# A fused attention and two-MLP kernel: the load of the third weight slice issued behind the first pair of heads' transposes

## Chip, cores and metric

One core of one Trainium2 chip runs the whole program as one launch. The metric is the device time of that launch in microseconds (us). Three runs of the kernel before gave 974.56, 975.61 and 974.90 us; the median is 974.9 us.

## What is computed

A causal attention with a learned decay (4 batches, 8 heads, 576 positions, head size 64) feeds an MLP with a squared relu (512 to 2048 and back), and that feeds a gated MLP (512 to 1536 and back), all in float32, with 2304 tokens:

```python
scores = scale * (q @ k.T)                       # per batch and head
cum    = cumsum(maximum(s, 0))
scores = where(causal, -1e9, scores + minimum(-(cum[:, None] - cum[None, :]), 0))
attn   = exp(scores - max(scores)); attn /= sum(attn) + 1e-9
x      = merge_heads(attn @ v)                   # 2304 x 512

h = maximum(x @ w_in, 0)
x = (s * h * h + b) @ w_out

out = ((x @ w_a) * (x @ w_b)) @ w2_out
```

The products keep float32 accuracy by splitting operands into a high and a low part and adding three products (high with high, high with low, low with high). Such splits are the bulk of the work of ScalarE (ACT) and VectorE (DVE).

## The kernel before

The program is written as a list of operations with an engine, a cost and a priority each (`Plan.op`, L79). `Plan.order` (L125) plays this list through with its own costs and writes out one fixed order, in which every engine then runs its instructions one behind the other. An operation can name others that it must be issued behind (`behind`, kept in the field `then`); it also becomes eligible only when its buffers have room. The buffers of one tag (`Tag`, L34) are handed out in the order in which they were declared, unless the tag says otherwise. A change to one operation can therefore move many others.

The first stretch, some 150 us, does two things at once.

**Attention, first halves.** Eight groups of four heads; group i is loaded by `light_load(i)` (L388): the keys and queries of the group (`kq`, two transfers of 64 x 1024, L411), its values (`rv`, L412) and two rows of running sums (L416). `first_half(i)` (L615) treats the group as two pairs of heads. For each pair, in two tiles of query rows (ti = 1 and 0): TensorE (PE) makes the scores `s` (L645), DVE their maximum `nm` (L650), ACT the exponentials `p` (L661), ACT and DVE the high and low part `hl` of the scaled probabilities (L555, L557), and a DMA transposes `hl` into `tr` (L671). One more PE operation, `av` (L595), multiplies `tr` with the values. ACT (L606) and DVE (L608) split its result into `x_all`. Names carry batch, pair and tile: `s0031` is the scores of batch 0, pair 3, tile 1, and `av003` and `tr003` belong to batch 0, pair 3. Groups 0 and 1 (`kq0`, `kq1`) are batch 0, groups 2 and 3 are batch 1.

**First MLP.** The weights come in 16 slices of 1 MB (`raw0` to `raw15`), loaded by `split_w` and `decode` (L479, L447, the load on L459). The inputs are 64-bit words; ACT and DVE put them together (L463, L468 or L472, L474), ACT or GpSimd (POOL) rounds to the high part (L483) and DVE makes the low part (L484). Only then can PE use a slice, in `h` (L934, which needs all four pairs of a batch) and `y` (L954).

Even slices and the early `kq` tiles share one tag, with 16 slots, in the order of declaration: `raw0`, then `raw2`, then `kq2`, `kq3`, then the first finished slice. Odd slices use a single buffer of their own, so slice f + 2 is loaded only when slice f is finished (odd f).

All transfers named here are issued by SyncE (SP), one behind the other, on one queue. Eight semaphores are used in turn: a transfer is issued only when the one issued eight places earlier has landed. The order on SP around the change is `raw0`, `raw1`, `raw2`, the loads of group 2, one load of group 3, and then the four transposes of the first two pairs.

Of the kernel before, what the change touches and what calls it, by code (L numbers as in the profile page):

```python
# [30 lines left out]
PE, DVE, ACT, POOL, SP = "PE", "DVE", "ACT", "POOL", "SP"  # L31
# [207 lines left out]
def fused_kernel(  # L239
# [15 lines left out]
    nc = tc.nc  # L255
# [12 lines left out]
    plan = Plan()  # L268
    op = plan.op
# [97 lines left out]
    def split_v(v3, rv, eng, cost, sub, pr):  # L367
# [11 lines left out]
           r=[rvb, (buf, 1)], w=[(buf, 2)])  # L379
        return ops  # L380

    light = {}
    casts = []
    last_rows = []
# [3 lines left out]
    def light_load(i, in_w):  # L388

        b, g = divmod(i, 2)  # L390
        kq = Buf(t_w if in_w else t_kq0, f"kq{i}")
        rv = Buf(t_rv0, f"rv0{i}")
        pr = 2.0 * i if i < 2 else light_pos(i) - 8.0
        vt = Buf(t_vt0, f"vt0{i}")
        light[i] = kq, rv, vt

        def view():
            a = kq.t.bitcast(F32).rearrange("p a b n -> p a (b n)") if in_w else kq.t.rearrange("p a x h n -> p a (x h n)")
            return a

        kq.view = view
        hs = slice(b * H + 4 * g, b * H + 4 * g + 4)

        def ones():
            nc.gpsimd.memset(view()[64:66, 1], 1.0 / SCALE)
            nc.gpsimd.memset(view()[64:66, 0], -1.0 / SCALE)

        op(POOL, 1.9, pr, ones, w=[(kq, "o0"), (kq, "o1")], behind=casts[2 * i - 3 : 2 * i - 2])
        for j, src in enumerate((kl, ql)):
            op(SP, 0.5, pr + 0.1 * j,  # L410
               lambda j=j, src=src: nc.sync.dma_start(view()[0:64, j], src[b, :, g]), w=[(kq, j)], dma=360000, behind=last_rows[-1:], slack=i > 1)  # L411
        op(SP, 0.45, pr + 0.3, lambda: nc.sync.dma_start(  # L412
            rv.t.rearrange("p x c h d -> p x (c h d)"), v[b, 2 * g : 2 * g + 2, :, :2].rearrange("x p c h d -> p x (c h d)")
        ), w=[rv], dma=262144, behind=last_rows[-1:] if i else (), slack=i > 1)
        for j, row in ((0, 64), (1, 65)):
            last_rows.append(op(SP, 0.6, pr + 0.4 + 0.1 * j, lambda j=j, row=row: nc.sync.dma_start(  # L416
                view()[row : row + 1, j].rearrange("p (h n) -> p h n", h=4), sums_ap()[hs, S : S + N]
            ), r=[(sums, "cum")], w=[(kq, f"o{j}")], dma=4096, behind=last_rows[-1:]))
        casts.extend(split_v((vt, lambda a: vt.t[..., a, :]), (rv, lambda: rv.t), POOL, 0.63, 0.7, light_pos(i) + (0.5 if i else 2.6)))

    def light_pos(i):
# [25 lines left out]
    def decode(raw, src, shift_on_act, pr, load_pr, later=()):  # L447
# [11 lines left out]
            nc.sync.dma_start(a, src.bitcast(U32))  # L459

        lo, hi, hi32 = (lambda: words(0)), (lambda: words(1)), (lambda: words(1).bitcast(F32))
        op(SP, 0.42, load_pr, load, w=[raw], dma=1 << 20, behind=later, slack=True)
        op(ACT, 1.07, pr, lambda: nc.scalar.activation(  # L463
            hi32(), hi32(), AF.Prelu, scale=2.0**-112, alpha=-(2.0**32)
        ), w=[(raw, "hi")])
# [149 lines left out]
    def first_half(i):  # L615
# [8 lines left out]
        for x in range(2):  # L624
# [41 lines left out]
            for ti in (1, 0):  # L666
                w, bank, at, view, hl = tiles[ti]
                for h in range(2):
                    split_p(hl, lambda hl=hl, h=h: hl.t.rearrange("p (k a h) n -> p k a h n", a=2, h=2)[:, :, :, h],
                            pts[ti, h], (rc, at + h), w, pr)  # L670
                op(SP, 1.25, pr, lambda ti=ti, tr=tr, hl=hl: nc.sync.dma_start_transpose(  # L671
                    out=tr.t.rearrange("p (k q) -> p k q", q=N)[:, : 4 * (ti + 1), (1 - ti) * P : (2 - ti) * P],
                    in_=hl.t.rearrange("p k n -> p (k n)"),
                ), r=[hl], w=[(tr, ti)], dma=49152 * 4 * (ti + 1), late=-0.9)
            value_product(b, 0, p, vt, lambda j, h, vi, x=x: vt.t[:, x, j, h, vi, :], tr, pr + 1.0)

    for i in range(2 * B):
        first_half(i)

    save_rows()  # L680

# [1020 lines left out]
```

## Time and profile before

| what | value |
|---|---|
| median of three runs | 974.9 us |
| the profiled execution, its own time | 973.57 us |
| its span (first to last instruction) | 971.7 us |
| PE busy | 940.7 us (97%) |
| DVE busy | 732.0 us (75%) |
| ACT busy | 560.8 us (58%) |
| POOL busy | 176.4 us (18%) |
| chain that ended last, by engine | PE 86%, DVE 6%, DMA 3%, ACT 2%, issue 2%, POOL 1% |
| PE busy in the first 48 us | 29.5 us |

How to read it: the span is 1.87 us shorter than the execution's own time, and that execution was 1.33 us faster than the median. PE is nearly always busy, so the end moves only if PE waits less, or runs the same work in less time. In the page's 40 slices PE shows 5 and 7 tenths in the first two and 9 tenths in nearly all others.

### The profile page before, as it was taken

To read this page: it belongs to the slowest core of one execution; us is meant where nothing else is said; L and a number is where in the kernel's file an instruction comes from. 1 tells how busy PE (TensorE), PEld (TensorE's weight loads), DVE (VectorE), ACT (ScalarE), POOL (GpSimd) and SP (SyncE) were. 2 spreads that over 40 slices of the span, in tenths; PEclk is the share of its full clock that TensorE was granted. 3 is DMA by queue.
4 is the path that set the end of the run, shared out by engine and by line. 5 is a ranking of instruction groups with operands and counts; after the bars stand their busy time and mean duration, and the time that the engine had idled before them with its cause. 6 is when DMAs were issued, how large, how long until landed. Compare 5 with 4: busy or idle time off the path is not lost.

```text
span 971.7 us, 16847 instructions
## 1 busy us (share of the span) xinstructions
PE 940.7 (97%) x6360; PEld 762.8 (78%) x6360; DVE 732.0 (75%) x1228; ACT 560.8 (58%) x1038; POOL 176.4 (18%) x234
## 2 busy tenths in 40 slices
PE   5799999999999999999999998999999999999998
PEld 4598999999999999999988884455554544788888
DVE  6889875767988988888559628868788786978852
ACT  4777864567878787887466425364455542334431
POOL 4124123210201102003032003141243410000000
PEclk9999999999999999999999999999999999999999
DMA  9969656347778887877352300445475668986022
GB/s 246 233 161 232 208 191 139 85 135 144 170 166 169 163 162 172 155 149 165 70 195 87 109 1 1 150 165 200 168 284 206 215 240 285 349 338 225 13 71 103
DMA packets 159857, 163.25 MB, mean 168 GB/s; under 512 B 115104, under 2 KB 125088, under 8 KB 153888
## 3 DMA queue, kind: packets, MB, share of 16 engines
q1 hardware_dynamic: 159776, 162.18, 58.9%
q8 instruction: 50, 0.82, 0.3%
q14 instruction: 31, 0.25, 0.1%
HBM read 99.39 MB, written 36.47 MB: 140 GB/s over the span
## 4 chain that ended last, share of the span: by engine, by line
PE 86%; DVE 6%; DMA 3%; ACT 2%; issue 2%; POOL 1%; SPq 0%; DVEq 0%; POOLq 0%; ACTq 0%
PE b L1245 21%; PE y L954 14%; PE h L934 14%; PE pb L1492 11%; PE yy L1002 5%; PE hh L990 4%; PE av L595 4%; PE s L645 3%; PE s L831 3%; PE bc L1245 3%; PE pbc L1552 2%; DMA tr<-hl 2%; DVE hl L557 1%; DMA raw<-in_w_dram 1%; DVE x L1176 0%
## 5 line engine op out<-in xcount | busy, mean ns | idle before, releaser
L954 PE MATMUL y<-g,w 128*128 128x256 f32 x1344 | 180.3, 286 | 0.2 <-ACT p L661 0.2
L934 PE MATMUL h<-x_all,w 128*128 128x256 f32 x1344 | 178.4, 286 | 1.9 <-DVE w L484 1.5
L934 PEld LDWEIGHTS h<-x_all,w 128*128 128x128 f32 x1344 | 168.0, 193 | 3.7 <-DVE w L484 2.6
L954 PEld LDWEIGHTS y<-g,w 128*128 128x128 f32 x1344 | 167.0, 191 | 2.8 <-ACT p L661 0.4
L1245 PEld LDWEIGHTS <-wa 128*128 128x128 f16 x720 | 70.0, 98 | 57.4 <-issue 3.2
L1245 PEld LDWEIGHTS <-ws 128*128 128x128 f16 x576 | 55.9, 98 | 66.9
L555 ACT ACTIVATE hl<-p,rc 128x256 f16<-128x256 f32 (+3 forms) x128 | 65.3, 557 | 25.9 <-DVE rc L572 9.9
L557 DVE SCALAR_TENSOR_TENSOR hl<-p,rc,hl 128x256 f16<-128x256 f32 (+3 forms) x128 | 73.6, 618 | 3.6 <-ACT hl L555 3.5
L1245 PE MATMUL b<-x,wa 128*128 128x512 f16 x288 | 68.7, 379 | 0.0
L884 ACT ACTIVATE r<-h 128x512 f32<-128x512 f32 x56 | 33.1, 591 | 51.3 <-PE h L934 50.4
L595 PE MATMUL av<-tr,vt 128*64 128x320 f16 (+4 forms) x800 | 48.1, 275 | 10.3 <-DMA tr<-hl 9.4
L595 PEld LDWEIGHTS <-vt 128*64 128x64 f16 (+1 forms) x800 | 40.5, 117 | 18.6 <-issue 7.5
L1492 PE MATMUL pb<-g,wo 128*128 128x512 f32 x216 | 50.9, 390 | 1.3 <-DVE g L1440 1.3
L645 PE MATMUL s<-kq 66*128 66x256 f32 (+1 forms) x128 | 42.4, 458 | 10.0 <-DMA kq<-sums 7.5
L1245 PE MATMUL b<-x0d,ws 128*128 128x512 f16 x216 | 50.9, 379 | 0.0
L1245 PE MATMUL b<-x1d,ws 128*128 128x512 f16 x216 | 50.9, 379 | 0.0
L895 DVE SCALAR_TENSOR_TENSOR r<-r,sb_s 128x512 f32<-128x512 f32 x40 | 30.3, 757 | 25.3 <-ACT r L884 24.8
L1492 PEld LDWEIGHTS pb<-g,wo 128*128 128x128 f32 x216 | 40.4, 188 | 10.1 <-DVE g L1440 1.7
L1286 DVE TENSOR_TENSOR su<-b,su 128x512 f32<-128x512 f32 x48 | 33.0, 687 | 18.4 <-PE b L1245 15.2
L1002 PE MATMUL yy<-gg,w 128*128 128x512 f32 x192 | 46.0, 390 | 0.0
L990 PE MATMUL hh<-x_all,w 128*128 128x512 f32 x192 | 46.0, 389 | 0.0
L1300 ACT COPY su<-b 128x512 f32<-128x512 f32 x24 | 14.0, 585 | 53.4 <-PE b L1245 50.2
(416 smaller groups left out, 1864.4 us busy)
## 6 DMA issues: line engine op xcount, KB each, us to landing
raw<-in_w_dram SPq DMA_DIRECT2D x16, 1024.0 KB
raw<-in_w2ab_dram SPq DMA_DIRECT2D x12, 1024.0 KB
ab_dr<-at_all SPq DMA_DIRECT2D x24, 512.0 KB
R<-ab_dr SPq DMA_DIRECT2D x24, 512.0 KB
wo<-wo_dr SPq DMA_DIRECT2D x12, 1024.0 KB
rk<-in_k_dram SPq DMA_DIRECT2D x16, 576.0 KB
raw_o<-in_w2o_dram SPq DMA_DIRECT2D x6, 1024.0 KB
wo_dr<-wao SPq DMA_DIRECT2D x24, 256.0 KB
```

The source lines that it names most:

```text
L555: nc.scalar.activation(o, i_, AF.Copy, scale=r_)
L557: nc.vector.scalar_tensor_tensor(out=o, in0=i_, scalar=r_, in1=place()[:, k0:k1, 0, :cols], op0=ALU.mult, op1=ALU.subtract)
L595: nc.tensor.matmul(ap.t[64 * h : 64 * h + 64, :w], vap(j, h, vi), t[:, j, a, h, :w], start=j == 0 and m == 0, stop=j == nkt - 1 and m == l ...
L645: nc.tensor.matmul(o, qt[:66, x, h, ti * P : (ti + 1) * P], kt[:66, x, h, :w], start=True, stop=False)
L884: op(ACT, 0.49, e, lambda: nc.scalar.activation(r.t.rearrange("p a n -> p (a n)"), hp.t, AF.Relu), r=[hp], w=[r], late=0.1)
L934: nc.tensor.matmul(o, w[:, wi, c, :], x_t[ck, c].t[:, xi], start=m == 0, stop=m == 3 * KC - 1)
L954: nc.tensor.matmul(o, w1_t[2 * fp + j].t[:, 1, wi, e * P : (e + 1) * P], g.t[:, gi, j], start=fp == 0 and e % 2 == 0 and j == wi == gi == ...
L990: nc.tensor.matmul(hp.t, w[:, wi, c, :], x_all[:, :, c, xi, :], start=m == 0, stop=m == 3 * KC - 1)
L1002: nc.tensor.matmul(y_ps[e].t, w1_t[f].t[:, 1, wi, e * P : (e + 1) * P], g.t[:, gi].rearrange("p a n -> p (a n)"), start=f == m == 0, stop= ...
L1245: nc.tensor.matmul(o, wt.t[:, q, wi, kt * P : (kt + 1) * P], hl_of(kt, xi), start=first and n == 0, stop=last and n == 5, skip_group_check ...
L1286: op(DVE, 0.64, e, lambda: nc.vector.tensor_tensor(out=dst(), in0=bank.t, in1=a(), op=ALU.add), r=[bank, *reads], w=[key], late=0.08)
L1492: nc.tensor.matmul(banks[bi][dp].t, wv(i2, wi, dp), hl.t[:, i2, xi, :], start=n_ in fresh and ip == i2 == m == 0, stop=ip == NIP - 1 and i ...
```

## The change

The issue of the load of `raw2` waits until the transpose of tile 0 of batch 0, pair 0 has been issued. The two dictionaries only keep hold of the operations; the loads of `kq` are recorded too, and nothing is done with them.

```diff
@@
+    loads, turns = {}, {}
@@ light_load
+        n0 = len(plan.ops)
         for j, src in enumerate((kl, ql)):
...
+        loads[f"kq{i}"] = plan.ops[n0:]
@@ decode
-        op(SP, 0.42, load_pr, load, w=[raw], dma=1 << 20, behind=later, slack=True)
+        loads[raw.name] = [op(SP, 0.42, load_pr, load, w=[raw], dma=1 << 20, behind=later, slack=True)]
@@ first_half
-                op(SP, 1.25, pr, lambda ti=ti, tr=tr, hl=hl: nc.sync.dma_start_transpose(
+                turns[b, p, ti] = op(SP, 1.25, pr, lambda ti=ti, tr=tr, hl=hl: nc.sync.dma_start_transpose(
@@
     for i in range(2 * B):
         first_half(i)
+
+    for name, p in (("raw2", 0), ):
+        for o in loads[name]:
+            turns[0, p, 0].then.append(o)
+            o.wait += 1
```

The order that the planner writes differs from there on, on every engine; on PE the two orders run alike again from about the thousandth row. Three places of it follow, before and after.

SP, from the first weight slice to the transposes of the second pair. Before:

```order
L459 DMA raw0_149<-in_w1_dram 128x2048
L459 DMA raw1_152<-in_w1_dram 128x2048
L459 DMA raw2_160<-in_w1_dram 128x2048
L411 DMA kq2_162<-in_kl_dram 64x1024
L411 DMA kq2_162<-in_ql_dram 64x1024
L412 DMA rv02_177<-in_v_dram 128x2x256
L416 DMA kq2_162<-sums_111 1x4x256 x2
L411 DMA kq3_224<-in_kl_dram 64x1024
L671 DMA_TRANSPOSE tr000_245<-hl0001_144 128x8x128
L671 DMA_TRANSPOSE tr000_245<-hl0000_155 128x4x128
L671 DMA_TRANSPOSE tr001_267<-hl0011_169 128x8x128
L671 DMA_TRANSPOSE tr001_267<-hl0010_180 128x4x128
```

With the change:

```order
L462 DMA raw0_149<-in_w1_dram 128x2048
L462 DMA raw1_152<-in_w1_dram 128x2048
L414 DMA rv02_160<-in_v_dram 128x2x256
L674 DMA_TRANSPOSE tr000_227<-hl0001_144 128x8x128
L674 DMA_TRANSPOSE tr000_227<-hl0000_155 128x4x128
L462 DMA raw2_245<-in_w1_dram 128x2048
L413 DMA kq2_247<-in_kl_dram 64x1024
L413 DMA kq2_247<-in_ql_dram 64x1024
L674 DMA_TRANSPOSE tr001_274<-hl0011_165 128x8x128
L674 DMA_TRANSPOSE tr001_274<-hl0010_173 128x4x128
L418 DMA kq2_247<-sums_111 1x4x256 x2
L413 DMA kq3_271<-in_kl_dram 64x1024
```

The third slice takes the keys and queries of group 2 with it, since their buffers stand behind its buffer in the shared tag; they now lie between the transposes of pair 0 and those of pair 1.

DVE, behind the low parts of pair 1. Before:

```order
L472 TENSOR_SCALAR raw2_160<-raw2_160 128x1024
L484 TENSOR_TENSOR w1_0_262<-raw0_149,w1_0_262 128x2x512
L571 TENSOR_SCALAR rc002_279<-sm002_253 128x4
L572 RECIPROCAL rc002_279<-rc002_279 128x4
L525 CAST sums_hl_282<-sums_111 32x576
L527 TENSOR_TENSOR sums_hl_282<-sums_111,sums_hl_282 32x576
L474 SCALAR_TENSOR_TENSOR raw1_152<-raw1_152 128x1024
L557 SCALAR_TENSOR_TENSOR hl0021_200<-p00210_252,rc002_279,hl0021_200 128x2x128
```

With the change:

```order
L653 TENSOR_REDUCE nm003_277<-s0031_253 128x2
L653 TENSOR_REDUCE nm003_277<-s0030_265 128x2
L657 TENSOR_SCALAR nm003_277<-nm003_277 128x4
L574 TENSOR_SCALAR rc002_311<-sm002_241 128x4
L575 RECIPROCAL rc002_311<-rc002_311 128x4
L487 TENSOR_TENSOR w1_0_309<-raw0_149,w1_0_309 128x2x512
L611 SCALAR_TENSOR_TENSOR x_all_82<-av000_283,x_all_82 128x256
L560 SCALAR_TENSOR_TENSOR hl0021_191<-p00210_240,rc002_311,hl0021_191 128x2x128
```

The maxima of pair 3 come ahead of the weight work; before they stood behind the low parts of pair 2, because PE made `s0030` only after `av000`. The steps on `raw1` and `raw2` go back.

PE, around the first `h`. Before:

```order
L595 MATMUL av100_574<-tr010_500,vt02_361 64x128
L934 MATMUL h0_0_597<-x_all_82,w1_0_262 128x256 x12
L934 MATMUL h0_0_597<-x_all_82,w1_1_363 128x256 x12
L645 MATMUL s0130_646<-kq3_224 128x128
L646 MATMUL s0130_646<-mask1_84,ident_83 128x128
```

With the change:

```order
L649 MATMUL s0120_524<-mask1_84,ident_83 128x128
L942 MATMUL h0_0_535<-x_all_82,w1_0_309 128x256 x12
L942 MATMUL h0_0_535<-x_all_82,w1_1_469 128x256 x12
L648 MATMUL s0131_611<-kq3_271 128x256
L649 MATMUL s0131_611<-mask1_84,ident_83 128x128
```

The first `h` stood behind all of `s0131` and `av100` before; now it stands behind `s0120`, ahead of both. In the whole order ahead of it, one score tile of 256 columns and one `av` are missing.

## Rows read from the trace of the kernel before

**Rows 1.** The page: busy time of each engine; granted clock in 40 slices.

```profile
PE 940.7 (97%) x6360; PEld 762.8 (78%) x6360; DVE 732.0 (75%) x1228; ACT 560.8 (58%) x1038; POOL 176.4 (18%) x234
...
PEclk9999999999999999999999999999999999999999
```

**Rows 2.** Windows: stretch, length, busy PE, PEld, DVE, ACT, POOL, clock, DMA share, GB/s.

```profile
14.00:16.00 2.00, 2.00 (x7) 1.73 (x7) 1.34 (x6) 0.56 (x2) 0.06 (x1) 1.00 1.00 422
...
24.00:36.00 12.00, 9.12 (x61) 8.05 (x61) 9.80 (x19) 8.88 (x25) 3.06 (x4) 1.00 0.80 162
36.00:48.00 12.00, 7.51 (x44) 5.94 (x44) 9.79 (x24) 9.48 (x29) 0.00 (x0) 1.00 1.03 299
48.00:60.00 12.00, 12.00 (x81) 10.87 (x78) 8.79 (x19) 6.38 (x18) 4.98 (x5) 1.00 0.83 209
60.00:72.00 12.00, 12.00 (x118) 11.32 (x117) 10.97 (x23) 11.86 (x28) 1.23 (x2) 1.00 0.38 111
72.00:84.00 12.00, 10.33 (x90) 9.48 (x89) 11.59 (x22) 7.20 (x28) 5.99 (x5) 1.00 0.91 208
84.00:96.00 12.00, 12.00 (x96) 11.79 (x96) 10.94 (x20) 11.06 (x27) 6.03 (x5) 1.00 0.87 239
```

**Rows 3.** Timeline of SP's queue: start, duration of the issue, line, transfer.

```profile
9.20 1.40 SPq L459 DMA_DIRECT2D raw<-in_w_dram  x3
10.64 0.66 SPq L411 DMA_DIRECT2D kq<-in_kl_dram  x1
...
19.30 1.36 SPq L671 DMA_TRANSPOSE tr<-hl  x1
...
23.50 2.14 SPq L671 DMA_TRANSPOSE tr<-hl  x1
...
40.05 4.28 SPq L671 DMA_TRANSPOSE tr<-hl  x2
```

**Rows 4.** Waits of SP's queue, first 60 us: total, times, longest.

```profile
SPq L671 <- DMA raw<-in_w_dram: 3.2, 3, 1.9
```

**Rows 5.** Chain that ended last: start, duration, what.

```profile
21.77 4.97 DMA tr<-hl
...
41.99 5.41 DMA tr<-hl
```

**Rows 6.** Timeline of PE: start, duration, operation, idle before and its releaser.

```profile
26.88 1.81 PE L595 MATMUL av<-tr,vt 128*64 128x256 f16 x20 [4.96 <-DMA tr<-hl]
...
30.09 1.81 PE L595 MATMUL av<-tr,vt 128*64 128x256 f16 x20
...
40.32 0.79 PE L645 MATMUL s<-kq 66*128 66x128 f32 x2 [0.94 <-DVE x_all L608]
...
47.54 1.81 PE L595 MATMUL av<-tr,vt 128*64 128x256 f16 x20 [3.55 <-DMA tr<-hl]
...
51.69 1.16 PE L645 MATMUL s<-kq 66*128 66x256 f32 x2
...
54.63 4.76 PE L934 MATMUL h<-x_all,w 128*128 128x256 f32 x24
...
61.42 1.02 PE L595 MATMUL av<-tr,vt 128*64 128x256 f16 x20
...
62.97 0.65 PE L645 MATMUL s<-kq 66*128 66x256 f32 x2
...
96.45 0.98 PE L954 MATMUL y<-g,w 128*128 128x256 f32 x6 [0.23 <-ACT p L661]
97.27 5.92 PE L934 MATMUL h<-x_all,w 128*128 128x256 f32 x48
```

**Rows 7.** Timeline of DVE.

```profile
56.10 1.22 DVE L484 TENSOR_TENSOR w<-raw,w 128x1024 fp32r<-128x1024 f32 x1
...
60.05 0.42 DVE L650 TENSOR_REDUCE nm<-s 128x2 f32<-128x256 f32 x1 [1.86 <-PE s L646]
...
96.12 2.35 DVE L484 TENSOR_TENSOR w<-raw,w 128x1024 fp32r<-128x1024 f32 x2
```

## The prediction, made before the changed kernel ran

> **What bounds the kernel now.** I read the page first: PE is busy for 97% of the span, and its granted clock reads full in every slice [rows 1]. Then the windows: of the 31 us in which PE does nothing, most lie ahead of 48 us (29.5 us busy of 48; the third and fourth 12 us have 9.12 and 7.51) [rows 2]. From there to 96 us PE is full but for 1.67 us, and DVE is nearly full as well: 33.50 of the 36 us from 60 to 96 [rows 2]. So this change can act in two ways: PE's early waits, and how soon DVE gets through its list.
>
> PE's timeline shows the early waits. `av000` stands 4.96 us for a transpose, a score tile 0.94 us for DVE, and `av003` 3.55 us for a transpose [rows 6]. It also shows that early PE work is slow, though the granted clock says 1.00 throughout [rows 1, 2]: the same score matmul takes 1.16 us for two at 51.7 and 0.65 us at 63.0, an `av` 1.81 and 1.02 us [rows 6]. That is the lower level (1.2 GHz) and the upper (2.4 GHz). The change falls inside the first 24 `h`, 54.63 to 59.2: 24 at the pace of the later ones (5.92 us for 48) would take 2.9 us, at half pace 5.8; they take 4.6 to 4.8, so the level rose some 3.5 to 4 us after the first `h` began [rows 6].
>
> Last, SP's queue and its waits: L671 waits 3.2 us for loads of raw weights, 1.9 at the longest [rows 4]. The first transpose goes out at 19.30 (over at 20.66), the second only at 21.77, the start of the 4.97 us of the chain that end with `av000` [rows 3, 5]. This is the wait that the change takes away.
>
> **The change, step by step.** Durations are from the profiled execution.
>
> *Transposes of pair 0.* The second no longer waits for `raw2`, so it starts at 20.66. With 4.97 us to landing [rows 5], `av000` starts at 25.6 instead of 26.88: 1.2 us. Alone this is worth nothing, since `av001` comes next.
>
> *Transposes of pair 1.* Ahead of them SP now also issues `raw2`, `kl` and `ql` of group 2: 0.47 (1.40 for three) and twice about 0.65 [rows 3]. From 21.9 that ends at 23.7, against 23.50 when pair 1's first transpose started before [rows 3]; its `hl` is ready by then either way. The second follows at 25.0 and lands after 4.97 to 5.41 us [rows 5], at 30.0 to 30.4; before, `av001` ran at 30.09 [rows 6]. Cost 0 to 0.3 us if the transfers ahead don't slow it (see the last rival).
>
> *Pair 3, the main gain.* `s0030` is now ahead of `av000`, at about 22 us in a gap in which PE waited anyway. So its maxima, exponentials and `hl` come early: `hl` is done soon after `av001` (ACT splits that result first: 31.8, then 1.9 us on ACT and DVE), at about 34. SP reaches the transposes of pair 3 behind those of pair 2 (32.0 to 33.3) and three small transfers, at 35.3; the second starts at 36.6 and lands 4.97 to 5.41 later, at about 42. Before, the second started at 41.99 and `av003` at 47.54 [rows 3, 5, 6]. PE, without a gap from 30, gets there at 42.5 (three score tiles of 256 columns at 2.1 us and two of 128 at 1.3, each twice a row like those at 51.69 and 40.32 with its mask and less the overlap, and two `av` at 1.75 [rows 6]). The waits of 0.94 and 3.55 us are gone.
>
> *The first `h`.* Behind `av003` (44.2) and one small tile (45.5) it starts at about 46 instead of 54.63, with one score tile and one `av` fewer ahead of it. If the clock again rises some 3.7 us into the `h`, these two run at the upper level: 2.13 against 1.14 us for the tile and 1.75 against 0.95 for `av`, 1.8 us saved. The 24 `h` end at 50.7, `s0131` at 51.8, and `av100` waits 0.6 us for its transpose, to 53.3. That is the work that PE had done at 59.2 before: 0.94 + 3.55 + 1.8 - 0.6 = **5.7 us ahead** on PE.
>
> *DVE takes most of it back.* Up to the low part of slice 7 (96.12 to 97.3, with PE's `h` on it at 97.27, just in time [rows 6, 7]) DVE's list has the same work in both orders, less two pieces of `hl` at 0.48 us. Following its list by the same durations, I get the 90th row done at 57.0, where before the 90th ended at 57.3 [rows 7]: the steps on slices 1 to 3 come later and wait behind ACT, which stands for `av001` and `av002`. So by then DVE has gained 0.3 us, not 5.7. From 57.3 to 97.3 it was idle some 4.4 us (2.5 of them from 60 to 96 [rows 2], and 1.86 for scores that PE had not made at 60.05 [rows 7]). With PE ahead, that 1.86 goes; what DVE waits for ACT (most of the rest) stays. Slice 7 is then ready 0.3 + 1.9 + 0.2 = 2.4 us earlier. Behind it, PE has six `y` more to do that it had done before (0.8 us, 96.45 to 97.27 [rows 6]). Slice 9 stands 17 rows behind slice 7 on DVE instead of 21, worth some 0.6 us of PE's small waits for slices up to 150 us. **Sum: 2.4 - 0.8 + 0.6 = 2.2 us.** After that both orders run alike and PE is full, so the lead stays. The bounds are 0 (DVE gains nothing) and 5.7 (PE keeps all its lead).
>
> The third slice itself costs nothing by coming late: PE needs it in `h` behind `av100`, 30 us on. The dictionaries add no instruction.
>
> The profiled execution becomes 973.57 - 2.2 = 971.4 us (span 969.5). It was 1.33 us faster than the median of 974.9, against which I forecast **972.7 us**. A measurement of this kernel can tell some 0.2%, 1.95 us, from no change; my forecast is just beyond.
>
> **A rule on the clock.** PE was busy without a gap from 26.88 to 39.3 on scores and `av`, and at 51.69 a score matmul still took the long time [rows 6]. The Trainium skill (TensorE: Matmul & The Clock Gate, section "What's actually happening") says that the throttled state is the default and that activity releases it. By that rule the gapless stretch from 30 us could bring the upper level before the first `h`, and most of the 12 us of PE work from 34 to 46 would take half its time. The row of 26.88 to 39.3 speaks against it, so the sum goes without it; it raises the chance of the first rival.
>
> **The rivals.**
>
> *PE's lead lasts: 969.2 us (0.14).* If DVE, ACT and PE together are what holds DVE back from 24 us on (10.1 us idle to 96 [rows 2]), an early PE lets DVE run closer to full and the whole 5.7 us reaches the end. For: DVE waits for PE in several places. Against: its first 90 rows gain nothing in my walk, and they contain the longest waits.
>
> *Nothing is left: 974.5 us, within 1.3 either way (0.18).* The change doesn't do what it says for PE: `raw2` was on nobody's path, and the wait that it caused was 1.1 us of `av000` only. The rearranged steps of slices 1, 3 and 5 come later (slice 1 some 7 us by my walk through the lists), and since an odd slice is loaded only when the last odd one is finished, the weights hold PE at 80 to 130 us by as much as it had won. For: PE's waits there are mostly for slices. Against: on DVE slice 7 and those behind it stand as early as before, or a few rows earlier.
>
> *Slower: 977.4 us, 976 to 979 (0.20).* `raw2` and the two loads of group 2 are 1.5 MB directly ahead of the transposes of pair 1. While weights were loaded the queue moved 422 GB/s [rows 2], so 1.5 MB are 3.6 us. If a transpose waits for all of it, pair 1 lands at 25.0 + 3.6 + 5.0 = 33.6 and `av001` is 3.5 us late. ACT has the split of `av001` ahead of `hl` of pair 3, so that slips too; the 90th row of DVE comes at 60.6, 3.3 late, and after 2.1 us of shorter waits and the 0.8 and 0.6 above, 1.4 us are lost by slice 7; the loads of slice 3 and 5, issued behind, lose about as much again. It decides if `av001` starts after 32.5. Against: the transposes of pair 3, from 41.99, landed 0.44 us later only (5.41 against 4.97) [rows 5] while the queue moved 299 GB/s [rows 2]. The Trainium skill (DMA: Bandwidth & Descriptors, section "Queues, rings and completion order") says that each DMA engine consumes descriptors in ring order. By that rule pair 1's transposes do wait for what is ahead.
>
> **How the numbers follow.** My forecast has 0.48, with a range of its own from 971.0 to 974.5; the rivals have 0.14, 0.18 and 0.20. Below 972.95 lie some 0.28 of my 0.48, all of the first rival and a little of the second: faster 0.44. Above 976.85 lie 0.18 of the last rival: slower 0.19 with a little from the second. The rest, 0.37, is the same. The range reaches from 969.3 to 977.2: it leaves out the lower half of the first rival and the upper half of the last.
>
> **What would show it.** Right: second transpose at about 20.7; `av003` at 42 to 43 without a wait; first `h` at 45 to 47 and its pace doubling within 4 us; PE idle less ahead of 48 us; DVE's low part of slice 7 at 94.5 to 95.5, with new or longer PE waits for slices between 55 and 95. Wrong: `av001` after 32.5 (last rival); matmuls at the short time before the first `h`; slice 7 before 93 (first rival) or at 97 and later (second).

## The result, and the profile after

The changed kernel takes **979.17 us**, median of eleven runs (977.00 to 982.89), against 974.9 us (eleven runs, 972.80 to 977.32): a ratio of **1.0054, 95% interval 1.0042 to 1.0066**, so slower by some 5 us. The forecast was 972.7 us, faster, with a range to 977.2. The profiled execution of the change is the slowest of its eleven: 982.89 us, span 981.1. Single rows below are read from it; sums over the whole span stand some 4 us above the median.

The page first, its busy times and the granted clock in 40 slices; they answer to [rows 1].

```profile
PE 944.5 (96%) x6360; PEld 766.9 (78%) x6360; DVE 731.9 (75%) x1228; ACT 561.1 (57%) x1038; POOL 175.0 (18%) x234
...
PEclk9989999899999999999999999999999999999999
```

DVE and ACT do the same work in the same time as before. PE is busy for 3.8 us more, and its granted clock isn't full in two slices, the third (about 49 to 74 us) and the eighth (about 172 to 196 us). The windows show where, in the columns of [rows 2] (stretch, length, busy PE, PEld, DVE, ACT, POOL, clock, DMA share, GB/s):

```profile
24.00:36.00 12.00, 5.09 (x44) 4.51 (x44) 7.73 (x21) 8.34 (x27) 0.61 (x1) 1.00 1.06 242
36.00:48.00 12.00, 11.35 (x67) 9.21 (x66) 8.06 (x18) 6.17 (x19) 2.96 (x4) 1.00 0.93 201
48.00:60.00 12.00, 10.28 (x69) 9.61 (x70) 9.68 (x22) 9.39 (x28) 3.48 (x4) 1.00 1.00 250
60.00:72.00 12.00, 11.35 (x91) 10.22 (x90) 11.34 (x24) 9.88 (x30) 2.31 (x3) 0.72 0.50 133
72.00:84.00 12.00, 9.15 (x85) 8.56 (x84) 11.93 (x19) 8.78 (x20) 5.41 (x6) 1.00 1.11 272
84.00:96.00 12.00, 11.22 (x91) 10.91 (x90) 9.47 (x18) 9.11 (x17) 3.29 (x3) 1.00 1.03 209
```

PE gains 3.84 us of busy time at 36 to 48 us and loses 4.03 at 24 to 36. From 48 to 84 us, where it had been full but for 1.67 us, it now idles 5.2 us, and at 60 to 72 us the granted clock is 0.72. PE's timeline names the waits, against [rows 6]:

```profile
24.92 1.81 PE L598 MATMUL av<-tr,vt 128*64 128x256 f16 x20 [1.36 <-ACT p L664]
...
45.54 1.81 PE L598 MATMUL av<-tr,vt 128*64 128x256 f16 x20
...
48.29 0.79 PE L648 MATMUL s<-kq 66*128 66x128 f32 x2 [0.94 <-DVE x_all L611]
...
49.63 4.74 PE L942 MATMUL h<-x_all,w 128*128 128x256 f32 x24
...
56.05 1.02 PE L598 MATMUL av<-tr,vt 128*64 128x256 f16 x20 [0.64 <-DMA tr<-hl]
...
60.95 2.50 PE L942 MATMUL h<-x_all,w 128*128 128x256 f32 x10 [0.65 <-DVE w L487]
63.38 1.81 PE L598 MATMUL av<-tr,vt 128*64 128x256 f16 x20
...
78.64 1.02 PE L598 MATMUL av<-tr,vt 128*64 128x256 f16 x20 [2.11 <-DMA tr<-hl]
```

`av000` and `av003` are early and the first `h` starts at 49.63 instead of 54.63, as forecast in kind. `av100` is done at 57.0, where PE had the same work done at 59.2 before: a lead of 2.2 us. But `av001` (the last line of the chain below) came at 32.72 instead of 30.09, and the lead is gone by 72 us, where PE has begun 21 `h` and `y` fewer than before: `h` on slice 2 waits at 60.95, and ten of its matmuls take 2.50 us, an `av` 1.81: the lower level again, up to 67 us. The timeline of SP and the chain show the start of it, against [rows 3, 5]:

```profile
9.20 0.92 SPq L462 DMA_DIRECT2D raw<-in_w_dram  x2
...
19.66 2.68 SPq L674 DMA_TRANSPOSE tr<-hl  x2
22.39 0.57 SPq L462 DMA_DIRECT2D raw<-in_w_dram  x1
23.02 0.54 SPq L413 DMA_DIRECT2D kq<-in_kl_dram  x1
23.61 0.59 SPq L413 DMA_DIRECT2D kq<-in_ql_dram  x1
24.30 2.98 SPq L674 DMA_TRANSPOSE tr<-hl  x2
```

```profile
25.77 6.82 DMA tr<-hl
32.58 0.14 issue
32.72 1.81 PE av L598 x20
```

Pair 1's second transpose takes 6.82 us from issue to landing, where the forecast had 4.97 to 5.41. And between the two raw loads at 9.20 and 22.39 us SP hands out little: the windows of DMA (last two columns: share, GB/s) of the changed kernel,

```profile
16.00:18.00 2.00, 2.00 (x10) 1.82 (x9) 1.18 (x4) 1.67 (x6) 1.64 (x3) 1.00 0.44 159
18.00:20.00 2.00, 0.49 (x4) 0.30 (x2) 1.58 (x5) 0.84 (x5) 2.00 (x3) 1.00 0.04 16
20.00:22.00 2.00, 2.00 (x6) 1.64 (x7) 1.86 (x7) 2.00 (x8) 0.59 (x1) 1.00 0.55 105
```

and of the kernel before, in the same stretch:

```profile
16.00:18.00 2.00, 2.00 (x9) 1.74 (x7) 0.86 (x2) 1.49 (x4) 1.94 (x3) 1.00 1.03 430
18.00:20.00 2.00, 0.49 (x2) 0.47 (x2) 1.94 (x7) 1.09 (x6) 0.45 (x1) 1.00 1.00 293
20.00:22.00 2.00, 1.92 (x6) 1.25 (x5) 1.85 (x5) 2.00 (x7) 0.00 (x0) 1.00 1.05 231
```

The DMA engines, full there before, stand idle for some 3.9 of these 6 us (2 x 0.56 + 2 x 0.96 + 2 x 0.45), and from 24 to 60 us their share in the change is 1.06, 0.93 and 1.00 (before: 0.80, 1.03 and 0.83 [rows 2]). The last view is DVE's waits from 24 to 57 us (us in total, times, longest), before:

```profile
DVE x_all L608 <- ACT x_all L606: 2.8, 2, 1.6
DVE rv L376 <- POOL vt L374: 1.4, 1, 1.4
DVE nm L650 <- PE s L646: 1.1, 2, 0.6
```

and after:

```profile
DVE x_all L611 <- ACT x_all L609: 5.3, 3, 3.3
DVE hl L560 <- ACT hl L558: 1.6, 1, 1.6
DVE nm L653 <- PE s L649: 1.5, 2, 0.9
DVE w L487 <- ACT w L486: 0.6, 1, 0.6
DVE rc L574 <- ACT p L664: 0.3, 1, 0.3
```

9.3 us instead of 5.3; the longest, 3.3, is the wait for `av001`. The low parts of slices 2 and 7 on DVE, which had started at 46.89 and 96.12:

```profile
59.67 1.23 DVE L487 TENSOR_TENSOR w<-raw,w 128x1024 fp32r<-128x1024 f32 x1 [0.62 <-ACT w L486]
...
99.96 2.35 DVE L487 TENSOR_TENSOR w<-raw,w 128x1024 fp32r<-128x1024 f32 x2
```

### The profile page after: what moved, and what is told of

It is laid out like the page before. It is cut to its first block, busy times and chain, and to the rows that moved or that the text cites. A ratio compares the mean times of both kernels' runs of the same rounds, so it can differ in the third digit from the quotient of the medians.

```text
span 981.1 us, 16852 instructions
## 1 busy us (share of the span) xinstructions
PE 944.5 (96%) x6360; PEld 766.9 (78%) x6360; DVE 731.9 (75%) x1228; ACT 561.1 (57%) x1038; POOL 175.0 (18%) x234
## 4 chain that ended last, share of the span: by engine, by line
PE 84%; DVE 5%; DMA 4%; issue 3%; ACT 3%; POOL 1%; SPq 0%; DVEq 0%; POOLq 0%; ACTq 0%
PE b L1253 20%; PE y L962 14%; PE h L942 14%; PE pb L1500 11%; PE yy L1010 4%; PE hh L998 4%; PE av L598 4%; PE bc L1253 3%; PE s L839 3%; PE s L648 2%; DMA tr<-hl 2%; PE pbc L1560 2%; DVE hl L560 1%; DMA y_dr<-yo 1%; DVE x L1184 0%
## 5 line engine op out<-in xcount | busy, mean ns | idle before, releaser
L962 PE MATMUL y<-g,w 128*128 128x256 f32 x1344 | 184.0, 289 | 0.0
L962 PEld LDWEIGHTS y<-g,w 128*128 128x128 f32 x1344 | 170.2, 194 | 2.0 <-issue 0.2
L560 DVE SCALAR_TENSOR_TENSOR hl<-p,rc,hl 128x256 f16<-128x256 f32 (+3 forms) x128 | 67.4, 572 | 4.3 <-ACT hl L558 4.3
L859 ACT ACTIVATE p<-s,nm 128x512 f32<-128x512 f32 (+1 forms) x64 | 40.4, 632 | 6.6 <-DVE nm L844 1.8
```

Source lines behind the costliest of these rows:

```text
L560: nc.vector.scalar_tensor_tensor(out=o, in0=i_, scalar=r_, in1=place()[:, k0:k1, 0, :cols], op0=ALU.mult, op1=ALU.subtract)
L859: nc.scalar.activation(pt.t[:, lo : lo + w], bank.t[:, :w], AF.Exp, bias=mm, scale=1.0, accum_out=sm.t[:, c : c + 1])
L962: nc.tensor.matmul(o, w1_t[2 * fp + j].t[:, 1, wi, e * P : (e + 1) * P], g.t[:, gi, j], start=fp == 0 and e % 2 == 0 and j == wi == gi == ...
```

## The experiments

The theories that were tried for the loss: E, it lies in the early part of the new order, and L, in the late part (behind some 105 us); D, it comes of the held-back loads of group 2, which leave the DMA engines without work; O, it comes of the changed order of the steps on the slices; C, it is the time at the lower clock at 60 to 67 us; S, it is the late slice 1 (and 3); P, it is the later place of slices 5 and 6; V, it is the early time that DVE loses. Their rival each time is that the loss lies elsewhere in the early order.

The planner writes a new order for every engine as soon as one edge is added, so that the change mixes what it says with what the planner makes of it. Most runs therefore take the order from a table: the operations are the same 3434 in all kernels, and only the order in which they are given to the engines is written out. A negative number only gives the operation its buffer at that place. `B` and `C` stand for the planner's orders of the kernel before and of the change.

```diff
     def emit(self):
-        for o in self.order():
+        for n in ORDER:
+            o = self.ops[abs(n)]
             for b in o.bufs:
                 if b.t is None:
                     b.t = b.tag.make(b.name)
-            o.fn()
+            if n >= 0:
+                o.fn()
```

All results in one table: median, ratio to the runs of the kernel before beside it, the `h` and `y` matmuls that PE had begun by 108 us (summed from their windows in the profile, without the matmuls that e_fill and b_pe_delay add; one is worth 5.92 / 48 = 0.12 us, and scores and `av` vary little), and the start of DVE's low part of slice 7.

| run | us | ratio, 95% interval | h and y by 108 us | slice 7 |
|---|---|---|---|---|
| before | 974.9 | | 306 | 96.1 |
| the change | 979.17 | 1.0054 (1.0042 to 1.0066) | 264 | 100.0 |
| early_only | 979.76 | 1.0054 (1.0036 to 1.0071) | 263 | 101.2 |
| late_only | 977.95 | 1.0024 (1.0009 to 1.0039) | 298 | 94.4 |
| p_raw2_tr0 | 974.23 | 0.9992 (0.9980 to 1.0004) | 307 | 96.2 |
| p_sp_order | 976.66 | 1.0019 (1.0010 to 1.0028) | 271 | 100.2 |
| p_kq_tr0 | 975.26 | 1.0003 (0.9992 to 1.0013) | 291 | 97.8 |
| e_kq_first | 977.01 | 1.0026 (1.0014 to 1.0038) | 277 | 99.5 |
| e_fill | 980.09 | 1.0053 (1.0038 to 1.0068) | 264 | 101.3 |
| b_slice1_late | 975.10 | 1.0002 (0.9993 to 1.0011) | 300 | 97.0 |
| e_slice13 | 979.45 | 1.0046 (1.0034 to 1.0059) | 269 | 100.7 |
| e_kq_slice13 | 976.57 | 1.0015 (1.0006 to 1.0025) | 291 | 97.5 |
| b_raw65 | 979.84 | 1.0058 (1.0046 to 1.0070) | 255 | 102.1 |
| e_all | 978.70 | 1.0040 (1.0028 to 1.0053) | 248 | 102.5 |
| e_raw | 980.59 | 1.0065 (1.0053 to 1.0078) | 249 | 102.4 |
| b_dve_delay | 975.62 | 1.0005 (0.9994 to 1.0016) | 286 | 99.0 |
| a_dve_delay | 980.23 | 1.0061 (1.0039 to 1.0083) | 260 | 100.2 |
| b_pe_delay | 981.29 | 1.0065 (1.0052 to 1.0078) | 252 | 102.5 |
| c_kq_first | 972.55 | 0.9960 (0.9945 to 0.9974) | 292 | 92.1 |
| b_kq_decl | 986.99 | 1.0137 (1.0112 to 1.0161) | 206 | 110.9 |

### Which part of the new order

The 422nd operation is about the load of `raw10`, issued at some 105 us; there the two orders have given out nearly the same work.

```diff
+ORDER = C[:422] + [n for n in B if n not in C[:422]]
```

> The operations come in a written-out order: the changed kernel's for the first 422 of 3434 (up to the load of raw10, issued at about 105 us), then the kernel before's. Theory L (the loss is made after 105 us, where the changed order puts the loads of vm later and the writes of y_dr behind them, and PE waits at 166 to 182 us): no stall at 173 us, 972 to 976 us, no slower than before. Theory E (the loss is made before 105 us: pair 1's transposes wait for what is queued ahead, av001 starts at 32.7, and the clock falls again at 61 to 67 us): 977 to 980 us, as slow as the changed kernel, and PE already behind at 100 us.

```diff
+ORDER = B[:422] + [n for n in C if n not in B[:422]]
```

> The other half: the order of the kernel before for the first 422 operations, the changed kernel's from there on. Theory L: PE waits some 3 us near 170 us for a copy of yo, whose place is held by a write of y_dr queued on SP behind a load of vm; the clock falls to the lower level behind it; 977 to 981 us. Theory E: 974 to 976 us, as before, with the early windows as before.

Theory L falls. The early part by itself costs as much as the whole change, 1.0054. The late part costs 2.3 us by itself, but nothing on top of the early one. In late_only PE does wait near 170 us, for a copy of `yo` that waits for a write of `y_dr` behind a load of `vm`:

```profile
168.47 0.49 PE L646 MATMUL s<-kq 66*128 66x128 f32 x2 [2.15 <-DVE x_all L609]
```

In return its slices are ready sooner (slice 7 at 94.4). The change's own profiled execution has the same wait, 3.22 us at 173.14; since early_only, without it, is as slow by its ratio, it isn't what made the change slow. That execution, the slowest of the eleven, also has a granted clock of 0.72 at 168 to 180 us; a_dve_delay, with the same order, has 1.00 there.

### The move by itself, and what it takes along

The kernel before, in its own order, with `raw2` alone moved; then with SP's whole order of the change up to pair 1; then with the loads of group 2 alone moved. The order on SP:

```diff
 p_raw2_tr0
-load raw2
 loads of group 2; kl of group 3
 transposes of pair 0
+load raw2
 transposes of pair 1
```

> The order of the kernel before, written out, with the load of raw2 alone moved behind the two transposes of pair 0 on SP (the loads of group 2 stay ahead of them), and DVE's first step on raw2 moved four rows of DVE back, behind the pieces of pair 2's hl. Second transpose at about 20.7, av000 at 25.6 to 26. Theory L: 974 to 976 us, the move alone is worth nothing either way. Theory E: the 1 MB of raw2 is now directly ahead of pair 1's transposes, which land 1 to 2.5 us later than before (av001 at 31 to 32.6), and 975 to 978 us.

```diff
 p_sp_order
-load raw2
-loads of group 2; kl of group 3
+rv of group 2
 transposes of pair 0
+load raw2
+kl, ql of group 2
 transposes of pair 1
+sums of group 2; kl of group 3
```

> As the run before it, but SP's whole order of the change up to pair 1: raw2 and both loads of group 2 (1.5 MB) stand between the transposes of pair 0 and those of pair 1; the orders of PE, ACT and DVE stay those of the kernel before but for that one step. Theory L: av001 late by 2 to 3 us, but DVE's list takes that up, 974 to 977 us. Theory E: av001 after 32.5 and 976 to 979 us.

```diff
 p_kq_tr0
 load raw2
-loads of group 2; kl of group 3
+rv of group 2
 transposes of pair 0
+kl, ql of group 2
 transposes of pair 1
+sums of group 2; kl of group 3
```

> The order of the kernel before with raw2 in its old place, and only the loads of group 2 (kl, ql) moved behind the transposes of pair 0, the rows of sums and the load of group 3 behind pair 1's: the opposite half of p_raw2_tr0 (974.2 us) out of p_sp_order (976.7 us). Theory D: the DMA engines now have raw2 until 20 us or so and lose some 0.5 to 0.75 MB of their work there, 1.2 to 1.8 us at 422 GB/s: 975 to 976.5 us. If instead raw2 ahead of pair 1's transposes were what makes p_sp_order slow: 974 to 975 us. If the loads of group 2 by themselves do it (their place among the 8 lanes of the queue): 976 to 977.5 us.

What the words of the change say, `raw2` behind pair 0's transposes, is worth nothing: 0.9992, though the first `av` comes at 23.91 instead of 26.88. Group 2's loads alone cost nothing to be seen either, 1.0003 (its 975.26 us lies between the forecasts of D and of the rival). Both together cost 1.9 us: only then does DMA have nothing to do for a while (its share at 18 to 20 us is 0.04, and 1.06 and 0.76 in the two others). Pair 1 lands late with 1.5 MB ahead of it and not with 1 MB. In p_raw2_tr0 and p_sp_order, the wait of PE for pair 1's second transpose:

```profile
29.50 1.81 PE L597 MATMUL av<-tr,vt 128*64 128x256 f16 x20 [2.31 <-DMA tr<-hl]
```

```profile
32.22 1.81 PE L597 MATMUL av<-tr,vt 128*64 128x256 f16 x20 [5.31 <-DMA tr<-hl]
```

and in the chain of p_sp_order the transpose itself, and a load of raw weights behind it:

```profile
25.64 6.45 DMA tr<-hl
...
40.11 9.09 DMA raw<-in_w_dram
```

In p_raw2_tr0 that transpose was issued at 24.74 us and landed after 4.63, in p_sp_order after 6.45. The chain goes on from there: SP issues the load of raw words at 40.11 instead of 37.94, ACT ends its steps on it at 51.36, and `av003` starts at 51.46 instead of 47.54. So in this run the delay goes through pair 1's transposes, which the held-back loads stand ahead of. What the idle time of DMA costs besides, by later loads, isn't separated from it.

The same from the other side: the change's early order with the loads of group 2 back in front.

```diff
 e_kq_first, against early_only
+loads of group 2; kl of group 3
-rv of group 2
 transposes of pair 0
 load raw2
-kl, ql of group 2
 transposes of pair 1
-sums of group 2; kl of group 3
```

> The run early_only (779 in hundredths: 979.8 us) with one thing changed: the loads of group 2 (kl, ql, the two rows of sums, 0.5 MB) and the first load of group 3 go out ahead of pair 0's transposes again, as in the kernel before; raw2 stays behind them, as in the change. PE, ACT and DVE keep the changed order. Theory D (what costs time is that the held-back loads leave the DMA engines without work from about 16 to 21 us, 0.67 busy share of the first 24 us against 0.95, and everything loaded up to 60 us, where they are full, comes some 4 us later): share of the first 24 us 0.85 to 0.9, the low part of slice 7 within 1.5 us of before (96.1), 973 to 976.5 us. Theory O (the changed order puts the steps on the slices behind attention's on ACT and DVE): slice 1's low part still at 40 us or later, slice 7 at 99 to 101, 978 to 980.5 us.

The share of DMA in the first 24 us is 0.91, the second transpose of pair 1 lands after 5.44 us, `av001` comes at 30.60, close to the forecast's 30.0 to 30.4, and the loss halves: 1.0026, between what D and O had expected. From p_raw2_tr0 to p_sp_order it is 0.27%, from e_kq_first to early_only 0.28%: once `raw2` is held back, holding the loads of group 2 back with it costs about **2.6 us** in either order. The intervals make that uncertain by some 1.5 us in the first pair and 2 us in the second, whose runs were also on two different chips. The other half, 2.5 us, is what is left in e_kq_first, and so lies in the rest of the new order.

### The clock

```diff
+                for _ in range(FILL.get((n, b.name), 0)):
+                    self.fill(b.t)
             o.fn()
...
+    plan.fill = lambda t: nc.tensor.matmul(t[:, :P], ident, mask1, start=True, stop=True)
...
+FILL = {(296, 'av100'): 14, (368, 's0201'): 5, (1522, 'h0_1'): 9, (365, 'av103'): 46}
```

> early_only with 74 small matmuls (128x128, into a bank that the next product overwrites) put into PE's waits at 55 to 61 us and ahead of the transpose wait at 75 us, so that PE has no gaps there. They compute nothing that is used. Theory C (the clock's fall to the lower level at 60.6 and 77 us, in the waits, is what costs time): granted clock 1.00 at 60 to 84 us, 975 to 977.5 us. Theory D or O: the clock stays up, but PE reaches the same waits for slices sooner, and 978 to 980.5 us.

```profile
60.00:72.00 12.00, 12.00 (x119) 11.18 (x119) 11.90 (x25) 10.51 (x33) 3.92 (x5) 1.00 0.63 173
72.00:84.00 12.00, 12.00 (x114) 11.73 (x113) 10.49 (x17) 7.59 (x19) 4.29 (x4) 1.00 0.98 231
84.00:96.00 12.00, 10.50 (x84) 10.10 (x82) 9.47 (x19) 8.63 (x16) 3.62 (x3) 1.00 0.96 220
```

The clock stays at 1.00 and PE is full to 84 us (early_only had 0.86 and 0.73 there), and nothing is won: 1.0053, and 264 `h` and `y` by 108 us against 263. PE then idles 1.5 us at 84 to 96 us. Theory C falls: in this order the fall of the clock takes time that PE would otherwise wait. The last 46 added matmuls may run past the wait that they fill (`av103` at 79.19, and at 78.22 in early_only), so that a gain of up to 1 us could be hidden.

### Slices

The chain of odd slices, which share one buffer of raw words, starts 9.7 us late in the change: slice 1's low part at 44.6 instead of 34.9. Three runs tried whether that is the other half.

```diff
 b_slice1_late, the kernel before; ACT and DVE
-second step, copy, or, low part of slice 1
 maxima and exponentials of s0100, s0110
+second step, copy, or, low part of slice 1
 SP
-load raw3
 transposes of pair 3
+load raw3
```

> The inverse, on the kernel before: its order everywhere, with only the four last steps on slice 1 put as far back among ACT's and DVE's steps as the change has them (its low part behind the maxima of s0110), and the load of raw3, which needs slice 1's buffer, behind pair 3's transposes on SP. Theory S: slice 1's low part at 42 to 46 us, raw3 issued at 44 to 48, slice 7 some 3 to 5 us late, 977 to 980 us, though no transpose and no other load is held back. If the chain of odd slices isn't the bound: 974 to 975.5 us.

```diff
 e_slice13, against early_only; ACT and DVE
+steps on slice 1
 split of av001
-steps on slice 1
+steps on slice 3
 pieces and scores of batch 1, pairs 2 and 3
-steps on slice 3
 SP
+load raw3
 load raw4
-load raw3
```

> early_only (979.8 us) with the steps on weight slices 1 and 3 moved forward in the written-out order, to about where the kernel before has them among attention's steps: on ACT and DVE the second step, the copy of the high part and the low part of each, and on SP the load of raw3 ahead of that of raw4. The loads of group 2 stay held back and DMA stays idle at 16 to 21 us. Theory S (the bound up to 150 us is the chain of odd slices, which share one buffer of raw words: low part, next load, its steps; the change starts that chain 9 us late, with slice 1's low part at 44 us instead of 34.9, and loses about 5 of them for good): slice 1's low part at 31 to 35 us, slice 7 at 97 to 99, 975.5 to 978 us. If only the idle time of DMA counts: 979 to 980.5 us.

The same moves on top of e_kq_first:

> The same moves on top of e_kq_first (977.0 us), where the loads of group 2 go first again: both suspected losses are taken away and the attention steps of PE, ACT and DVE keep the changed order, with pair 3 early. Theory S and D together: slice 7 at 94 to 97 us, 972.5 to 975.5 us, no slower than before. If the changed order of attention itself costs: 976 us or more.

Theory S falls by b_slice1_late: slice 1's low part at 43.5 us and 1.0002. e_slice13 brings slice 1 back to 34.2 us and stays at 1.0046; slices 5 to 7 are within 0.5 us of early_only. On e_kq_first the moves may bring some 1 us, with intervals that overlap; the 976.57 us lie on the side of "the changed order of attention itself costs".

Slices 5 and 6 come next. In the change SP hands out their loads at 65.3 us and behind, behind transposes that wait for attention until 62.7; before, at 49.2 and 57.4. e_all and e_raw move them and their steps forward by hand (on e_kq_slice13 and e_slice13), b_raw65 moves them back in the kernel before.

```diff
 e_all, e_raw; SP
+load raw6
+load raw5
 transposes of batch 1's pair 2
-load raw6
-load raw5
...
 ACT and DVE
+steps on slices 5 and 6, some ten rows forward
```

> e_kq_slice13 (976.6 us) with one thing more: on SP the loads of raw6 and raw5 ahead of the two transposes of batch 1's pair 2, and that of raw7 ahead of batch 2's pair 0, where the kernel before has them, and the steps on slices 5 and 6 on ACT and DVE moved forward by some ten rows. Theory P (in the changed order these loads stand behind transposes that wait for attention until 62 us, with the DMA engines idle at 61 to 63 us): raw6 and raw5 issued before 60 us, slices 5 and 6 at 76 to 80 us, slice 7 at 93 to 96, 973 to 975.5 us. If the place of these loads is not it: 976 to 977.5 us.

> The same moves on e_slice13 (979.5 us), where the loads of group 2 are still held back and DMA is idle at 16 to 21 us. Theory P with D: the idle stretch at 16 to 21 us remains, slice 7 at 96 to 98 us, 976 to 978 us, some 2.5 us above e_all. If only the place of the loads counts: 974 to 975.5 us. If it doesn't count: 979 to 980.5 us.

```diff
 b_raw65, the kernel before; SP
-load raw6
-load raw5
 transposes of batch 1's pair 2
+load raw6
+load raw5
 ACT and DVE
-steps on slices 5 and 6
+steps on slices 5 and 6, in the change's rows
```

> The inverse, on the kernel before: its order, with the loads of raw6 and raw5 behind the transposes of batch 1's pair 2 on SP, as the change has them, and the steps on slices 5 and 6 on ACT and DVE moved back to the change's rows (otherwise those engines would block on them; PE's two h steps on slices 5 and 6 change places with that). Nothing is held back at the start. Theory P: raw6 issued at 67 to 69 us instead of 49.2, raw5 behind it, slices 5 and 6 at 83 to 86 us, 977 to 979.5 us. If the place of the loads doesn't count: 974 to 976 us.

b_raw65 is as slow as the change, 1.0058, with nothing held back at the start:

```profile
64.73 2.60 SPq L673 DMA_TRANSPOSE tr<-hl  x2
67.38 1.06 SPq L461 DMA_DIRECT2D raw<-in_w_dram  x2
```

So this place of slices 5 and 6 is enough to lose 5 us. That it is what makes the second half in the change isn't shown: in e_all and e_raw the loads go out at 55 to 62 us, but the steps, where I had put them, hold up attention on ACT and DVE (SP's next four transposes last from 61.36 to 71.74 us in e_all), slice 7 comes at 102.5 and both are slower, not faster. Theory P has one side of its proof and missed on the other.

### Whose time it is

```diff
 b_dve_delay, a_dve_delay
-            o.fn()
+            for _ in range(1 + 4 * (o.n == 553)):
+                o.fn()
```

> The kernel before, with one DVE step at 26.4 us (the low part of sums_hl, 0.75 us, whose repetition writes the same values) done five times instead of once: DVE is held 2.6 us longer, nothing else is changed. Theory V (up to slice 7, at 96 us, DVE's list is the bound, and what it idles in the first 60 us comes out at the end; the change lets DVE idle 3.7 us more between 24 and 96 us): slice 7 at 97 to 98.7 us, 976 to 978 us. If DVE's early time isn't the bound: 974 to 975.5 us.

> The changed kernel with the same step done five times: there it stands directly ahead of the 3.32 us that DVE waits for av001, so the 2.6 us fill idle time. Theory V: as the change itself, 978.5 to 980 us (with b_dve_delay at 976 to 978, the difference between the two kernels shrinks from 4.3 to about 2 us). If DVE's steps weren't the bound, or the wait weren't idle time that the change adds: both move alike, by 0 or by 2 us.

```diff
 b_pe_delay
+            if o.n == 1515:
+                for _ in range(28):
+                    self.fill(o.bufs[-1].t)
             o.fn()
```

> The kernel before with 28 small matmuls (128x128, into the bank that the next product overwrites) ahead of the first h at 54.6 us, where PE has no gap: PE falls some 3 us behind there. Theory V: PE catches up in the 1.7 us of gaps and where it waits for slices up to 150 us, slice 7 within 0.7 us of 96.1, 974 to 976 us: PE's lead or lag at 57 us is worth little, which is why the lead that the change gives to PE came to nothing. If PE is the bound from 48 us on: 977 to 978.5 us.

Theory V holds up to slice 7 and falls as to the end. The step done five times took 3.87 us instead of 0.75. These 3.1 us taken from DVE at 26 us make slice 7 2.9 us late and cost 1.0005: `av` of batch 1's pair 3 runs 2.9 us late (81.02 against 78.14), the next one, at 155 us, only 1.65. PE has 2.3 us of gaps between 96 and 180 us in the kernel before and 1.3 in b_dve_delay, so a part is caught up there. The change bears the same 3.1 us as well (1.0061 with a wide interval, against 1.0054). PE's time is another matter: the 28 matmuls took 6.24 us at the lower level, twice what I had priced, and 6.3 us were lost, all of it.

```profile
54.60 6.24 PE L346 MATMUL h<-mask,ident 128*128 128x128 f32 x28
```

```profile
60.00:72.00 12.00, 12.00 (x90) 11.68 (x91) 5.12 (x11) 6.07 (x13) 0.61 (x1) 1.00 0.18 71
```

In the second line, 60 to 72 us of that run, DVE and ACT are half idle (before: 10.97 and 11.86 busy [rows 2]): their lists wait for PE there, and so slices 4 to 7 come 6.3 us late as well. Why the gaps behind 96 us, 2.2 us in that run, take up nothing of this lag isn't shown.

### A version that is faster than both

```diff
-    for f in range(3):
+    for f in range(2):
         raw_of(f)
     for i in range(2, 4):
         light_load(i, True)
+    raw_of(2)
```

With this edit on the change, holding `raw2` no longer holds the loads of group 2, since the third slice's buffer stands behind theirs:

> The change itself, ordered by the planner, but with the weight pool's third slice declared behind groups 2 and 3, so that holding raw2 back no longer holds back their loads. Theory D: busy share of DMA in the first 24 us 0.85 to 0.95 and 972 to 976 us. Theory O: 976 to 980 us.

> Control for c_kq_first (972.6 us): the kernel before with the third slice declared behind groups 2 and 3 in the weight pool, and no load held back. If c_kq_first gains from the hold: 974 to 976 us here. If it gains from the declaration, which lets the planner order the loads anew: 971.5 to 973.5 us here too.

c_kq_first takes 972.55 us, 0.9960: by the ratios it is 3.9 us faster than the kernel before and some 9 us faster than the change. The control shows that the edit alone, without the hold, is 13 us slower than the kernel before. Both have new orders throughout, so this is one good order that the planner happened to find, not a price for the edit or the hold. Its profiled execution was the slowest of its ten (974.01 us) and no faster than that of the kernel before (973.57 us), so that its trace doesn't show where the gain lies. Its waits on PE from 24 to 83 us are

```profile
30.00 1.81 PE L599 MATMUL av<-tr,vt 128*64 128x256 f16 x20 [7.90 <-DMA tr<-hl]
42.65 1.81 PE L599 MATMUL av<-tr,vt 128*64 128x256 f16 x20 [1.88 <-POOL kq L407]
48.48 1.81 PE L599 MATMUL av<-tr,vt 128*64 128x256 f16 x20 [0.42 <-DMA tr<-hl]
...
78.47 1.45 PE L943 MATMUL h<-x_all,w 128*128 128x256 f32 x10 [0.62 <-DVE w L487]
```

The fastest kernel of all waits 7.90 us for the very transposes that the change hurries (4.96 before), and then PE has 1.4 us of gaps from 49 to 84 us (5.2 from 48 to 84 in the change).

## Why the prediction was wrong

- *The transposes of pair 0.* Right: both are out by 22.3 us and `av000` starts at 24.92 (forecast 25.6). That this alone is worth nothing was right too (p_raw2_tr0).
- *The transposes of pair 1: the first step that failed.* "Cost 0 to 0.3 us if the transfers ahead don't slow it": they did. `av001` came at 32.72 (31.98 in a_dve_delay and 32.16 in early_only, which have the same order there), not 30.0 to 30.4; the last rival had named 32.5. The sum counted SP's time for issuing the moved loads, and left to that rival that they are 1.5 MB which DMA can't carry while they are held, from 16 to 21 us, and then has ahead of pair 1. The step is worth 2.6 us, by two pairs of runs. The Trainium skill (DMA: Bandwidth & Descriptors, section "Queues, rings and completion order") has it that a DMA engine consumes descriptors in ring order. The 6.82 us with 1.5 MB ahead fit that; the 4.63 us with 1 MB ahead (p_raw2_tr0) show no wait for it.
- *Pair 3 and the first `h`.* Right in mechanism: `av003` has no wait of its own any more. It runs at 45.54, not 42.5, by `av001`'s delay; the 0.94 us wait for DVE stayed, ahead of another score tile; `h` starts at 49.63, not 46. PE's lead at `av100` was 2.2 us, not 5.7. One reading of the rows before was a little off: by the two paces of `h`, 0.25 and 0.12 us each, the level rose 3.3 to 3.7 us into them, not 3.5 to 4; nothing hangs on it.
- *DVE: the second step that failed.* "I get the 90th row done at 57.0". It was done at 60.90, almost what the last rival said (60.6): 9.3 us of waits ahead of 57 us in place of 5.3. Behind it the forecast said that 1.86 us of waiting for scores would go and the waits for ACT would stay. The waits for scores went, but DVE now waited 2.4 us for ACT's step on slice 7's words. Slice 7 was ready at 101.2, not 94.9. I had followed DVE's list by its durations and not asked whether the loads of slices 3 to 7 and ACT's steps on them come in time on their own queues.
- *What slice 7 is worth.* Its time was the right thing to watch, but the price wasn't one to one: 2.9 us late cost nothing to be seen in b_dve_delay. What the change does between 57 and 108 us is lose on PE: 6.1 us of waits (0.8 up to 60 us, 0.65, 2.85, 0.78 and 1.01 in the windows of 12 us behind) against 1.9, and at 60 to 72 us 12 x 0.28 = 3.4 us by the clock; less the lead of 2.2 that is 5.4 us, and the 42 `h` and `y` fewer by 108 us are 5.2. By e_fill the clock's share would have been lost in waits anyway.
- *"After that both orders run alike".* They don't, up to about 200 us; the late part by itself costs 1.0024. It didn't add to the loss.
- *The rivals.* The last one (0.20) had the mechanism and the sign, and with 977.4 us (976 to 979) too small a price: it is p_sp_order, 976.66. The second (0.18), that `raw2` was on nobody's path, holds for `raw2` alone. Its remark that slices 1, 3 and 5 come later was right, but slice 1, made as late in the kernel before, cost nothing (b_slice1_late).

What stays open is which rows of the new order make the second half, 2.5 us. A late slice 1 doesn't (b_slice1_late), the clock doesn't (e_fill), DVE's early time doesn't (b_dve_delay). The place of slices 5 and 6 is enough to lose as much and more (b_raw65), but taking it away didn't bring it back (e_all), by an order that was mine and not good.

## What to carry to other kernels

When one load is held back, look at what stands behind it for the same pool or queue, and at whether the DMA engines have other work in the meantime: here the load that was meant cost nothing, and the two that went with it cost some 2.6 us more: DMA had nothing to do while all three were held, and then had them to carry ahead of the next pair's transposes. A wait at the start of an engine that isn't full there can be worth nothing by itself (`av000` 2.97 us earlier in p_raw2_tr0: 0.9992); price an edit by the first stretch in which the engine is full, and ask of each list (DVE, ACT, SP) whether its inputs come in time, not only how long its rows take. Where a planner orders the work, write its order out as a table and move one thing at a time, since an edit of a few lines gives a new order throughout: three of them were worth -4, +5 and +13 us here.

## What the runs showed of the hardware that I had not expected

- The clock fell again after it had risen. After the `h` at 49.63 to 54.2 us PE ran scores and one `av` with waits of 0.64, 0.41, 0.38 and 0.65 us, and from 60.6 to 67 us matmuls took twice as long, with the granted clock at 0.50. With the 74 small matmuls of e_fill in these waits it stayed at 1.00 (0.12 us for each of the 46 at 73.96). The other way round it didn't rise: PE had no gap from 32.72 to 47 us in the change, and the 24 `h` at 49.63 still took 4.74 us (4.76 before). Nor did it rise in the 6.24 us of 28 matmuls of 128 columns in b_pe_delay: 0.22 us each, all at the lower level, and the `h` behind them still needed 5.10 us for 24. The Trainium skill (TensorE: Matmul & The Clock Gate, section "What's actually happening") says that activity releases the throttle. In these rows the level rose during the `h`, and in none of the stretches of scores, `av` and mask products ahead of them, however gapless.
- 1 MB directly ahead of two transposes on SP's queue didn't delay them to be seen: the second landed 4.63 us (p_raw2_tr0) and 5.44 us (e_kq_first) after its issue, against 4.97 and 5.41 in the kernel before. 1.5 MB did: 6.45 us (p_sp_order) and 6.82 us (the change).
- The kernel before varies from 972.3 to 977.8 us between executions, and the intervals of the ratios are some 1 us wide to either side, so that effects under 1 us stay open here.
